# Earlier first loads, quarter folds and respaced folds in a fused attention and feed-forward kernel

## The chip, the cores and the metric

The kernel runs on one core of a Trainium2 chip. The metric is the device time of one execution in microseconds (us), taken as the median of several. A profile of one execution goes with each run; its span is about 1.8 us shorter than the time. All executions used here are with a granted TensorE clock of 0.99 to 1.00 of full speed.

## The reference

For each of four batches, `q`, `k`, `v` are 5824 x 256. The channels attend to each other, and the result goes through a multiplicative feed-forward layer:

```python
qn = q / (norm(q, axis=1) + 1e-6);  kn = k / (norm(k, axis=1) + 1e-6)
a  = softmax(kn.T @ qn / tau)            # 256 x 256 per batch
x  = v @ a                               # 5824 x 256
out = ((x @ w1) * (x @ w2)) @ w3 @ w_out # w1, w2: 256 x 1024, w3: 1024 x 1024, w_out: 1024 x 256
```

## The kernel before

No `x` is made. `a` is folded into the weights, `Wf = a @ [w1, w2]` (eight "folds" of 512 columns per batch), and `W = w3 @ w_out` is made once (eight "w products"). Then each step is two products with v transposed, a cast by ScalarE, a multiplication by VectorE and the product with `W`. A chunk is eight steps over 512 rows; a batch has eleven full chunks and a small last one of 192 rows.

The softmax of batch n+1 needs all of its q and k. Their products (`G`) and square sums are spread between the steps of batch n; for batch 0 they stand at the start, behind the loads. An agenda says at which time of a modelled clock each piece of such side work is put between steps:

```python
def fold_mm(i, c2, tag="ab", on_act=None):        # one fold: matmuls c2 = 0 and 1, then its evacuation
    ...
    dst = Wf[n][:, c1, w, h * 512 : (h + 1) * 512]
    if on_act if on_act is not None else i % 2 == 0:
        nc.scalar.activation(out=dst, in_=st["fold", i], func=AF.Copy, scale=st["rs"][:, c1 : c1 + 1])
    else:
        nc.vector.tensor_scalar_mul(dst, st["fold", i], st["rs"][:, c1 : c1 + 1])
...
+ [(0.2, 15.5, sums)]                              # cost, time after the end of the products
+ [(0.43, 16.5 + 0.85 * i, lambda i=i: fold(i)) for i in range(8)]
...
# start of the program
busy(14)                                           # dummy matmuls
load_piece("k", 0, 0, (half,))                     # all loads by GpSimd, which casts to bf16
load_piece("q", 0, 0, (half,))
...
# agenda of batch b
for jt in range(FT):
    at(26.0 + 1.2 * jt, 0.87, lambda jt=jt: w_unit(jt))     # w products, batch 0 only
...
t0, t1 = 57.0, 115.5      # batch 0: products of the next batch from t0 to t1
t0, t1 = 16.0, 104.0      # later batches
```

Folds and the step products `a` and `b` share four PSUM buffers (`tag="ab"`).

## Time and profile before

| | before |
|---|---|
| time, median of the runs beside the change | 573.16 us |
| span of the profile | 571.7 us |
| TensorE busy | 559.4 us (98%) |
| last k piece of batch 0 lets TensorE go | 31.53 us |
| first real step product | 40.69 us |

The useful reading here is of what TensorE does *not* do. I call a hole the distance between the starts of two successive matmuls, less what the first needs (columns / 2.4 GHz + 2.5 ns, as the prediction has it; 215.8 ns for 512 columns, where the trace has 216.5). Summed by stage, holes tell where time is lost even when the busy share reads 98%. The prediction below shows the lines.

### The profile page before, as it was taken

How to read it: one execution, taken by the hardware profiler on the slowest of the kernel's cores; microseconds unless marked ns; L12 is line 12 of the kernel's file. 1: busy time of each engine (PE TensorE's matmuls, PEld its weight loads, DVE VectorE, ACT ScalarE, POOL GpSimd, SP SyncE). 2: the span in 40 equal slices, each digit the busy share in tenths (PEclk: the TensorE clock that was granted, in tenths of full speed). 3: DMA queues.
4: the chain of work that ended last, by engine and by line, in shares of the span. 5: the costliest groups of instructions: out<-in, count | busy, mean ns of one | idle time of the engine just before them, and what ended most of it. 6: DMA issues, size and time to landing. Idle time of an engine off the chain costs nothing.

```text
span 571.7 us, 10102 instructions
## 1 busy us (share of the span) xinstructions
PE 559.4 (98%) x3750; PEld 354.5 (62%) x3750; DVE 377.4 (66%) x612; ACT 337.7 (59%) x624; POOL 83.3 (15%) x164
## 2 busy tenths in 40 slices
PE   7789999999999999999999999999999999999997
PEld 4655576776666666666666666666665666666665
DVE  1047744788977567887776667778876656565564
ACT  0046644777856567776766567767766554454453
POOL 5250020303030111121030012031120000000000
PEclk9999999999999999999999999999999999999999
DMA  8999959869685697495661595665640325221011
GB/s 163 211 187 208 184 104 240 170 149 242 140 183 118 123 204 150 94 192 121 145 144 72 99 215 123 140 136 126 175 110 38 85 73 148 63 63 75 38 72 58
DMA packets 74560, 76.93 MB, mean 135 GB/s; under 512 B 54160, under 2 KB 58256, under 8 KB 74512
## 3 DMA queue, kind: packets, MB, share of 16 engines
q0 software_dynamic: 15504, 39.46, 39.3%
q1 hardware_dynamic: 58784, 36.64, 22.2%
q8 instruction: 29, 0.48, 0.3%
q10 hardware_dynamic: 224, 0.20, 0.1%
q14 instruction: 19, 0.16, 0.1%
HBM read 78.91 MB, written 23.86 MB: 180 GB/s over the span
## 4 chain that ended last, share of the span: by engine, by line
PE 92%; DMA 5%; DVE 1%; ACT 1%; POOL 1%; issue 0%; ACTq 0%; POOLq 0%
PE o L479 28%; PE a L438 27%; PE b L438 27%; PE G L188 5%; DMA k<-in_k_dram 5%; PE fold L349 2%; PE w L596 1%; ACT as L444 0%; ACT kr L279 0%; POOL k L109 0%; POOL q L109 0%; DVE abs L453 0%; PE sqk L221 0%; DVE vT L136 0%; DVE abs L455 0%
## 5 line engine op out<-in xcount | busy, mean ns | idle before, releaser
L453 DVE TENSOR_TENSOR abs<-as,b 128x512 bf16<-128x512 bf16 x336 | 230.5, 687 | 141.4 <-ACT as L444 130.3
L444 ACT CAST as<-a 128x512 bf16<-128x512 f32 (+1 forms) x384 | 216.1, 563 | 176.9 <-DVE abs L453 90.2
L438 PEld LDWEIGHTS <-Wf 128*128 128x128 bf16 x1536 | 149.2, 98 | 102.0 <-issue 1.9
L479 PE MATMUL o<-W_sb,abs 128*128 128x256 bf16 x1376 | 209.6, 273 | 0.1
L438 PE MATMUL a<-vT,Wf 128*128 128x512 bf16 x704 | 209.4, 379 | 0.2
L438 PE MATMUL b<-vT,Wf 128*128 128x512 bf16 x704 | 209.3, 379 | 0.0
L479 PEld LDWEIGHTS <-abs 128*128 128x128 bf16 x1376 | 134.5, 98 | 81.6 <-DVE abs L455 0.3
L197 DVE TENSOR_TENSOR acc<-acc,sq 128x1024 f32<-128x1024 f32 x66 | 80.4, 1219 | 0.4 <-ACT sq L185 0.3
L188 PE MATMUL G<-k,q 128*128 128x256 bf16 x276 | 49.9, 273 | 0.0
L185 ACT ACTIVATE sq<-q 128x512 f32<-128x512 bf16 x66 | 41.8, 634 | 0.0
L185 ACT ACTIVATE sq<-k 128x512 f32<-128x512 bf16 x66 | 41.6, 630 | 0.0
L426 POOL COPY gate_t<-abs 1x1 bf16<-1x1 bf16 x39 | 13.9, 355 | 167.7 <-DVE abs L453 167.0
L500 DVE COPY osb<-o 128x512 f32<-128x512 f32 x44 | 30.1, 685 | 0.7 <-PE o L479 0.7
L430 POOL COPY gate_t<-vT 1x1 bf16<-1x1 bf16 x17 | 4.4, 258 | 169.3 <-DMA vT<-v 134.0
L188 PEld LDWEIGHTS <-q 128*128 128x128 bf16 x276 | 27.0, 98 | 3.1
L499 ACT COPY osb<-o 128x512 f32<-128x512 f32 x44 | 25.8, 586 | 3.8 <-PE o L479 1.8
L279 ACT ACTIVATE kr<-row 128x256 f32<-128x256 f32 x1 | 0.4, 385 | 31.6 <-PE row L267 31.6
L109 POOL DMA_DIRECT2D q<-in_q_dram x29 | 15.7, 541 | 13.2 <-DMA k<-in_k_dram 6.0
L349 PE MATMUL fold<-w,e 128*128 128x512 bf16 x64 | 17.0, 380 | 0.5 <-DVE vT L136 0.4
L356 ACT ACTIVATE Wf<-fold,rs 128x512 bf16<-128x512 f32 x16 | 10.9, 688 | 8.1 <-PE fold L349 6.4
L244 DVE TENSOR_TENSOR dk<-sqk,ident 128x256 f32<-128x256 f32 x1 | 0.4, 425 | 21.3 <-PE sqk L221 21.3
L109 POOL DMA_DIRECT2D k<-in_k_dram x25 | 13.8, 551 | 3.7 <-DMA k<-in_k_dram 1.9
(89 smaller groups left out, 240.4 us busy)
## 6 DMA issues: line engine op xcount, KB each, us to landing
out_dram<-osb SPq DMA_DIRECT2D x44, 512.0 KB, 3.1
k<-in_k_dram POOLq DMA_DIRECT2D x19, 512.0 KB, 8.5
v<-in_v_dram POOLq DMA_DIRECT2D x19, 512.0 KB, 5.2
q<-in_q_dram POOLq DMA_DIRECT2D x18, 512.0 KB, 6.6
w_wout<-in_moe_w_dram POOLq DMA_DIRECT2D x1, 2048.0 KB, 23.6
k<-in_k_dram POOLq DMA_DIRECT2D x4, 320.0 KB, 9.9
v<-in_v_dram POOLq DMA_DIRECT2D x4, 320.0 KB, 5.4
q<-in_q_dram POOLq DMA_DIRECT2D x4, 256.0 KB, 12.0
```

The costliest lines, as they stand in the source:

```text
L109: nc.gpsimd.dma_start(out=pieces[nm, n, pi][:, lo:hi, :], in_=qk_main[nm, n][0][:, pi * PIECE + lo : pi * PIECE + hi, :])
L185: nc.scalar.activation(out=dst[:, :, part, :], in_=src[:, o : o + 2, :], func=AF.Square)
L188: nc.tensor.matmul(G[:, ct, :], lhsT=qt[:, i, ct * P : (ct + 1) * P], rhs=kt[:, i, :], start=(pr == 0 and part == 0 and ct == 0), stop=(pr ...
L197: nc.vector.tensor_add(accs[n], accs[n], sqs[0])
L349: nc.tensor.matmul(st["fold", i], lhsT=st["e"][:, c2, c1 * P : (c1 + 1) * P], rhs=w12[:, c2, w, h * 512 : (h + 1) * 512], start=(c2 == 0), ...
L426: nc.gpsimd.tensor_copy(gate_t, last_ab[0][:1, :1])
L438: nc.tensor.matmul(t[:, :n], lhsT=Wf[b][:, ct, w, j * P : (j + 1) * P], rhs=rhs_of(b, c, ct), start=(ct == 0), stop=(ct == CT - 1),)
L444: nc.scalar.copy(a_sb[:, :n], tiles[0][:, :n])
L453: nc.vector.tensor_mul(ab, a_sb, tiles[1])
L479: nc.tensor.matmul(tl[h][:, o, :], lhsT=lhsT, rhs=W_sb[:, j, :], start=(j == 0 and o == 0), stop=(j == FT - 1 and (small or o == 1)), skip ...
L499: nc.scalar.copy(o[:, 0:2, :], tl[0])
L500: nc.vector.tensor_copy(o[:, 2:4, :], tl[1])
```

## The change

Its intent: start the first loads earlier by giving half a piece of k and of q to SyncE, which is idle; fold only the columns that the first steps need before the first step and the rest between steps; load q and k of batch 1 earlier; and spread the folds at each change of batch so that their evacuations do not pile up. The core of the diff, condensed:

```diff
-            sum_mm(0) ... fold_mm(0..1), fold(2), transpose, fold(3), fold(4), fold(5)
+            sum_mm(0); quarters of columns 0:256 (both w, both c1); sum_mm(1)   # evacuated 128 columns at a time
+        def second_quarter(): ...                  # columns 256:512, after the first step
-            + [(0.2, 15.5, sums)]
-            + [(0.43, 16.5 + 0.85 * i, lambda i=i: fold(i)) for i in range(8)]
+            + [(0.2, 16.5, sums)]
+            + [(0.43, 17.5 + 1.1 * i, lambda i=i: fold(i)) for i in range(8)]
...
-    busy(14)
-    load_piece("k", 0, 0, (half,))
-    load_piece("q", 0, 0, (half,))
+    busy(10)
+    for nm in "kq":
+        new_piece(nm, 0, 0)
+        raw[nm] = work.tile([P, half, C], F32, tag="o_sb", name=f"raw_{nm}", bufs=3)
+        nc.sync.dma_start(out=raw[nm], in_=qk_main[nm, 0][0][:, :half, :])
+        load_part(nm, 0, 0, half, PIECE)
...
+    nc.vector.tensor_copy(pieces["k", 0, 0][:, :half, :], raw["k"])
+    nc.scalar.copy(pieces["q", 0, 0][:, :half, :], raw["q"])
...  # v first half piece, then w1 and w2 in columns 0:256, 256:512, 512:1024 (before: halves)
-    busy(4)
+    busy(3)
+    transpose_half_on_pe(0, 0, 0, False)
...
-                at(1.5 + 0.6 * i, 0.43, soft0[5 + i])
+            at(0.5, 0.87, soft0[5]);  at((1.7, 2.6, 3.5, 3.9)[i], 0.43, soft0[6 + i])
...  # moves: ("qk", 1, 0) at 29 ahead of ("v", 0, 3), ("qk", 1, 2) at 47, v(1, 0..2) 2 earlier
-            t0, t1 = 57.0, 115.5
+            t0, t1 = 54.0, 113.0
-            t0, t1 = 16.0, 104.0
+            t0, t1 = 16.0, 98.0
```

## The prediction

> **What bounds the kernel now.** I read the page first: the busy shares, the slices, and the chain that ended last.
>
> ```profile
> PE 559.4 (98%) x3750; PEld 354.5 (62%) x3750; DVE 377.4 (66%) x612; ACT 337.7 (59%) x624; POOL 83.3 (15%) x164
> ...
> PE   7789999999999999999999999999999999999997
> ...
> PEclk9999999999999999999999999999999999999999
> ...
> PE 92%; DMA 5%; DVE 1%; ACT 1%; POOL 1%; issue 0%; ACTq 0%; POOLq 0%
> ```
>
> TensorE is busy 98% of 571.7 us at full granted clock, and only the first three slices (43 us) and the last show slack. So any gain must come out of TensorE's few holes. To size them I took the start of each matmul in the timeline and subtracted the spacing that the one before needs. In full flow two 512-column matmuls start 0.433 us apart, so 0.2165 us each. The excess over that spacing sums to 13.1 us: 9.5 before 40 us, 0.95 at the first change of batch (175 to 182 us), 0.60 at the second (303 to 315), 1.47 at the third (436 to 448), 0.6 at the very end, and zero in every 10 us bucket between. So 3.0 us lie in the three changes and the rest in the start.
>
> The timeline of the start shows what holds it:
>
> ```profile
> 1.22 1.23 POOL L109 DMA_DIRECT2D k<-in_k_dram  x2 [0.78 <-POOLq L692]
> ...
> 31.53 0.84 PE L221 MATMUL sqk<-k 128*128 128x128 bf16 x12 [0.18 <-DMA k<-in_k_dram]
> ...
> 34.74 1.03 PE L209 MATMUL warm_I-482_483<-warm 128*128 128x512 bf16 x4
> ...
> 37.02 0.20 PE L328 MATMUL sum<-ones_b,e 128*128 128x1 bf16 x2 [1.25 <-ACT e L318]
> ...
> 40.69 0.59 PE L438 MATMUL a<-vT,Wf 128*128 128x512 bf16 x2
> ```
>
> GpSimd issues the first load at 1.22 us; the last k piece of batch 0 lets TensorE go at 31.53; the squares and products of what was left run to 34.7; four dummy matmuls and a wait fill the softmax chain to 37.02; six folds and one transpose of v run to 40.69, where the first real product starts. Windows of 2 to 4 us give the load's pace:
>
> ```profile
> 2.00:4.00 2.00, 2.00 (x6) 0.76 (x5) 0.00 (x0) 0.01 (x1) 2.00 (x5) 1.00 0.66 76
> 4.00:6.00 2.00, 2.00 (x9) 0.70 (x7) 0.00 (x0) 0.00 (x0) 2.00 (x5) 1.00 1.11 203
> ...
> 16.00:20.00 4.00, 2.14 (x26) 1.58 (x23) 0.00 (x0) 0.00 (x0) 0.56 (x1) 1.00 1.06 214
> ```
>
> The last two columns are DMA share and GB/s landed (bf16; twice that is read as fp32). From 4 to 28 us the rate is flat at 203 to 221, the DMA share over 1: the load is limited by transfer, not by issue or by TensorE. Summing packets gives 110 KiB landed at 4 us and 5257 KiB at 29, which is 206 KiB/us; that line drawn back meets zero at 3.48 us. So the load behaves as if it began at 3.48 us, and an earlier start moves the whole front end earlier.
>
> The third change of batch, the worst, in the timeline:
>
> ```profile
> 438.29 1.65 PE L349 MATMUL fold<-w,e 128*128 128x512 bf16 x6
> ...
> 446.60 0.33 PE L438 MATMUL a<-vTt,Wf 128*128 128x192 bf16 x2 [0.27 <-ACT as L444]
> ```
>
> Three folds back to back (six matmuls) come here and again 3 us later; this run takes 1.78 us from its start to the next matmul (438.29 to 440.07) where 6 x 0.2165 = 1.30 would do. Each fold must be evacuated (0.69 us on ScalarE, 0.75 on VectorE) from four shared PSUM buffers, and the backlog reaches the small last chunk, where TensorE needs less time per step than ScalarE and VectorE.
>
> **What the Trainium skill says.** "DMA: Bandwidth & Descriptors", section SWDGE vs HWDGE vs iDMA: casting in a DMA is GpSimd's alone. Hence raw fp32 by SyncE needs a cast on VectorE and ScalarE; no trace before shows that. Its Specifications give first-byte latencies of about 1 us (GpSimd) and 0.6 us (SyncE). The trace agrees in order, not in size: GpSimd's first issue at 1.22 has its first packet at 2.60 (1.38 us); SyncE's last full output store, issued at 564.40, has its first at 565.23 (0.83) and its last, of 512 KiB, at 566.66. Same page, Issuing engines are not separate DMA queues: all use the same 16 engines, so a second issuer adds no bandwidth. I take that as it stands: I credit the earlier start, not a higher rate. "TensorE: Matmul & The Clock Gate", section Wait — 56ns, not 53.3ns?: N / 2.4 GHz plus about 2.5 ns per matmul, 215.8 ns for 512 columns; the trace has 216.5.
>
> **The change part by part.**
>
> 1. First half pieces of k and q by SyncE. In the trace SyncE is released at 0.65 us and then has nothing to do. Issuing at about 0.7, plus 0.83, gives packets from about 1.55 us, 512 KiB of source in about 1.4 us. It fills the hole before 3.48: effective start 1.6 to 2.2 instead of 3.48, so 1.3 to 1.9 us less. The two casts (1024 columns; a VectorE add of that width is 1.22 us, a ScalarE copy 1.01) run while TensorE waits for loads, so they cost nothing. Credit: **-1.5 us**, for everything up to the last k piece. Ten warm-up matmuls instead of 14 lie under the load as well: 0.
>
> 2. Quarters first. TensorE's work is the same (eight 512-column matmuls become sixteen of 256: 8 x 2.5 ns more); only idle and filler count. Before, from 34.74 to 40.69: filler 4 x 0.2165 = 0.87, then a hole of 1.41 to 37.02, 0.1 at the sums, 0.51 at the fold that waited behind VectorE's vT copy: 2.9 us. After: filler 0.65, the v transpose (0.45) moved into the hole, which leaves 1.18, 0.1, and then TensorE has nothing to do between the last first-quarter matmul (about 38.0) and the first evacuated column block. That block needs the reciprocal sums (38.11 before) plus 0.07 plus one evacuation of 256 elements (about 0.45, from 0.69 for 512 and 0.42 for 256 columns on ScalarE), so 38.65: 0.65. Sum 2.6: **-0.3 us**. The first real product itself starts about two microseconds earlier, but work it jumped over comes back.
>
> 3. That work, the second quarter and folds 4 to 7, now lies between the first four product steps. I stepped the four PSUM buffers through with as 0.59, product 0.69, folds 0.69 and 0.75 us. Fold 7 waits about 0.3 us for a buffer, and product step 4, whose columns start at 512, waits about 0.5 for fold 7's evacuation. **+0.8 us**; before had no hole there. The w1, w2 quarters have the same bytes ahead of them as the halves had, so they should land in time with about half a microsecond to spare.
>
> 4. Folds spread, products of batches 1 and 2 ending at 98 instead of 104. The new order of instructions, which I built but did not run, has at the second and third change all eight folds inside the last full chunk, in pairs, with a product step between pairs and one after the sums; none stays for the small chunk. At the first change they go mostly one by one through the last chunk, with no run of three at the end. Of 3.0 us I keep 0.8 (0.18 at the leftover rows stays): **-2.2 us**. VectorE has room: the products get 82 clock units instead of 88, so its adds rise 7% where it is busy 74% (89.78 of 121.1 us, 182 to 303).
>
> 5. q and k of batch 1 ahead of late v: v piece 3 was transposed by 82.66 us and is first used at 107.04 us; a load of two pieces in front costs about 5 us of that 24. Piece 4: 105.4 against 139.6. The transfers stay hidden: **0**.
>
> Sum: -1.5 - 0.3 + 0.8 - 2.2 = **-3.2 us**. 572.96 - 3.2 = 569.8 us.
>
> **Rivals.** (a) The SyncE start gains nothing, because startup latency or a shared limit holds the first packets: for it, nobody has seen SyncE's first load here; against it, SyncE idle from 0.65 and a DMA hole until 3.5. Then 571.3. (b) Four PSUM buffers turn the early interleaved folds into holes of 2 us or more, as the runs of three do at the third change, or the w quarters with their short rows land late (the rate sinks to 131 to 188 KiB/us while short pieces land at 30 to 33 us): then 571 to 571.5. (c) The folds only move their holes into the last full chunk: gain there 0.5, total 571.5. (d) Everything works better, early holes near zero and changes of batch clean: 568.3. (e) A late v or q stalls a whole chunk: slower by several us; the slacks under 5 speak against it.
>
> **Range and chances.** Two rivals at once give about 572.5, the good case 568.3. Runs agree within 0.1% apart from one of 575.41 in three. I say 569.8, range 568.2 to 571.8. Two per cent is 11.5 us; the whole slack is 13.1 plus 1.5 of filler, much of it needed, so faster by that is all but excluded, and slower needs a stall that nothing shows.
>
> **What would show it.** Step 1: the last k piece releases TensorE near 30.0 instead of 31.53, first packets at 1.5 to 1.6. Step 2: the first product near 37.1 us (38.65 less 1.5) instead of 40.69. Step 3: waits of folds or products for evacuation between 39 and 46 us, near 0.8 us. Step 4: excess spacing at the three changes near 0.8 in total. Step 5: no TensorE wait for vT. The prediction is wrong if the load's end does not move, if the early holes pass 2 us, or if new holes open in mid-batch.

## The result, and the profile after

The changed kernel takes 572.23 us (median of six, 571.62 to 573.43) against 573.16 beside it. The ratio is 0.9979, 95% interval 0.996 to 0.9997. (Ratios are the mean time of one kernel's runs over that of the other's of the same rounds, so not quite the ratio of the medians quoted.) The gain is 0.9 us where I had forecast 3.2, and the time is above my range. In the changed kernel L438 has become L463, L479 L504 and L349 L350. First, three lines of its page: busy times and the chain that ended last.

```profile
PE 558.5 (98%) x3753; PEld 354.8 (62%) x3753; DVE 377.7 (66%) x613; ACT 339.9 (60%) x627; POOL 77.5 (14%) x164
...
PE 91%; DMA 6%; ACT 1%; DVE 1%; issue 0%; POOL 0%; ACTq 0%; POOLq 0%
PE o L504 27%; PE a L463 27%; PE b L463 27%; PE G L188 5%; DMA k<-in_k_dram 5%; PE fold L350 2%; DMA w3T<-w_wout 1%; PE w L627 1%; ACT as L469 1%; PE quarter L376 0%; ACT kr L279 0%; POOL k L109 0%; DVE s L313 0%; ACT e L318 0%; DVE abs L478 0%
```

The same bound, but a new item in the chain, `DMA w3T<-w_wout`: the transposes of w3, on nobody's path before. The timeline of the start:

```profile
0.73 0.40 SPq L542 DMA_DIRECT2D raw_k<-in_k_dram  x1
...
30.63 0.84 PE L221 MATMUL sqk<-k 128*128 128x128 bf16 x12 [0.17 <-DMA k<-in_k_dram]
...
35.88 0.20 PE L328 MATMUL sum<-ones_b,e 128*128 128x1 bf16 x2 [0.77 <-ACT e L318]
...
37.59 0.61 PE L463 MATMUL a<-vT,Wf 128*128 128x512 bf16 x2 [0.56 <-DVE Wf L387]
```

The last k piece lets TensorE go 0.90 us earlier, and the first step product starts 3.1 us earlier. The lead is spent later. The table gives the holes by stage for every profile; "early" runs from the first step product to the w products, "1st", "2nd" and "3rd" are the changes of batch. In some profiles a few matmul records are missing; each missing fold matmul (0.216 us) is taken out of the holes, and so are the four one-column matmuls of the sums at each change (0.09 us).

| run | last k | first step | early | w products | 1st | 2nd | 3rd | span | median time |
|---|---|---|---|---|---|---|---|---|---|
| before | 31.53 | 40.69 | 0.00 | 0.00 | 0.94 | 0.60 | 1.48 | 571.7 | 573.16 |
| changed | 30.63 | 37.59 | 0.25 | 0.65 | 1.60 | 0.24 | 0.60 | 570.5 | 572.23 |
| e1 SyncE alone | 30.97 | 39.61 | 0.12 | 0.00 | 0.94 | 0.60 | 1.19 | 570.3 | 572.26 |
| e2 dummy first | 31.49 | 40.64 | 0.00 | 0.00 | 0.94 | 0.60 | 1.47 | 571.5 | 572.96 |
| e3 w late | 30.87 | 37.89 | 0.21 | 0.00 | 1.60 | 0.24 | 0.60 | 570.0 | 572.04 |
| e4 products to 105 | 30.50 | 37.46 | 0.21 | 0.08 | 0.60 | 0.37 | 0.60 | 578.4 | 577.22 |
| e5 w late, old batch 0 | 30.50 | 37.46 | 0.22 | 0.00 | 1.90 | 0.24 | 0.61 | 569.9 | 571.92 |
| e6 without SyncE | 31.52 | 38.55 | 0.08 | 0.00 | 1.60 | 0.25 | 0.60 | 570.7 | 572.75 |
| e7 fold times alone | 31.43 | 40.46 | 0.00 | 0.00 | 0.36 | 0.42 | 0.60 | 569.7 | 571.49 |
| e8 w1, w2 in halves | 30.89 | 37.95 | 0.21 | 0.00 | 1.60 | 0.24 | 0.61 | 570.2 | 573.06 |
| e9 folds deferred | 30.24 | 37.68 | 0.22 | 0.08 | 3.12 | 0.47 | 0.61 | 571.9 | 572.41 |
| e10 folds at end, v later | 30.60 | 38.10 | 0.21 | 0.00 | 0.36 | 0.24 | 0.61 | 569.0 | 570.49 |
| e11 SyncE and fold times | 30.70 | 39.65 | 0.12 | 0.00 | 0.36 | 0.24 | 0.61 | 568.8 | 571.46 |
| e12 folds at end | 30.57 | 37.53 | 0.21 | 0.00 | 0.36 | 0.24 | 0.60 | 568.5 | 570.50 |
| e13 folds alone later | 30.35 | 37.77 | 0.21 | 0.00 | 0.76 | 0.24 | 0.61 | 569.1 | 571.04 |
| e14 folds at end, halves | 30.44 | 38.26 | 0.21 | 0.00 | 0.36 | 0.24 | 0.61 | 569.2 | 571.24 |

Every profile has 0.60 us more at the end of the last batch. The holes and the release by the last k piece repeat well between profiles except where a transfer is involved: the last k piece varies from 30.24 to 30.97 in the twelve runs with SyncE (mean 30.6; 31.5 in the four without), and in e9, e10 and e13 a q piece comes later still and costs 0.6 us. The medians are of four different rounds; the kernel before beside them had 573.01 to 573.55.

The third change of the changed kernel, to be compared with the run of three in the prediction: four matmuls, 4 x 0.2165 = 0.87 us, and the next product after 0.87.

```profile
436.90 1.03 PE L350 MATMUL fold<-w,e 128*128 128x512 bf16 x4
437.77 0.59 PE L463 MATMUL a<-vT,Wf 128*128 128x512 bf16 x2
```

The balance of the change in its profile: last k piece -0.90; from there to the first step, holes and filler from 3.25 to 2.76, -0.49; early +0.25; w products +0.65; changes of batch +0.66, -0.36, -0.88. Sum -1.1 us; the spans differ by 1.2.

### The profile page after: what moved, and what is told of

It reads as the page before. It is cut to its first block, busy times and chain, and to the rows that moved or that the text cites. A ratio compares the mean times of both kernels' runs of the same rounds, so it can differ in the third digit from the quotient of the medians.

```text
span 570.5 us, 10131 instructions
## 1 busy us (share of the span) xinstructions
PE 558.5 (98%) x3753; PEld 354.8 (62%) x3753; DVE 377.7 (66%) x613; ACT 339.9 (60%) x627; POOL 77.5 (14%) x164
## 4 chain that ended last, share of the span: by engine, by line
PE 91%; DMA 6%; ACT 1%; DVE 1%; issue 0%; POOL 0%; ACTq 0%; POOLq 0%
PE o L504 27%; PE a L463 27%; PE b L463 27%; PE G L188 5%; DMA k<-in_k_dram 5%; PE fold L350 2%; DMA w3T<-w_wout 1%; PE w L627 1%; ACT as L469 1%; PE quarter L376 0%; ACT kr L279 0%; POOL k L109 0%; DVE s L313 0%; ACT e L318 0%; DVE abs L478 0%
## 5 line engine op out<-in xcount | busy, mean ns | idle before, releaser
L463 PEld LDWEIGHTS <-Wf 128*128 128x128 bf16 x1536 | 149.0, 98 | 102.8 <-issue 2.3
L463 PE MATMUL a<-vT,Wf 128*128 128x512 bf16 x704 | 209.4, 379 | 0.8 <-DVE Wf L387 0.6
L504 PE MATMUL o<-W_sb,abs 128*128 128x256 bf16 x1376 | 209.9, 273 | 0.1
L463 PE MATMUL b<-vT,Wf 128*128 128x512 bf16 x704 | 209.4, 379 | 0.0
L504 PEld LDWEIGHTS <-abs 128*128 128x128 bf16 x1376 | 134.5, 98 | 81.9 <-DVE abs L480 0.3
L451 POOL COPY gate_t<-abs 1x1 bf16<-1x1 bf16 x39 | 9.6, 246 | 171.8 <-DVE abs L478 171.0
L350 PE MATMUL fold<-w,e 128*128 128x512 bf16 x56 | 15.0, 379 | 0.2 <-ACT as L469 0.2
L478 DVE TENSOR_TENSOR abq<-as,b 128x512 bf16<-128x512 bf16 x16 | 10.8, 687 | 5.2 <-ACT as L469 4.6
```

The lines of the kernel that those rows point to most:

```text
L350: nc.tensor.matmul(m, lhsT=st["e"][:, c2, c1 * P : (c1 + 1) * P], rhs=w12[:, c2, w, lo:hi], start=(c2 == 0), stop=(c2 == CT - 1),)
L463: nc.tensor.matmul(t[:, :n], lhsT=Wf[b][:, ct, w, j * P : (j + 1) * P], rhs=rhs_of(b, c, ct), start=(ct == 0), stop=(ct == CT - 1),)
L478: nc.vector.tensor_mul(ab, a_sb, tiles[1])
L504: nc.tensor.matmul(tl[h][:, o, :], lhsT=lhsT, rhs=W_sb[:, j, :], start=(j == 0 and o == 0), stop=(j == FT - 1 and (small or o == 1)), skip ...
```

## The experiments

Edits are shown condensed. The w products first, for the new item in the chain. What TensorE's weight loads waited for in the changed kernel (time in all, times, longest), and a piece of its chain in order of time:

```profile
PEld L627 <- DMA w3T<-w_wout: 1.3, 2, 0.7
```

```profile
62.53 5.76 DMA w3T<-w_wout
68.29 0.04 issue
68.34 1.92 PE w L627 x16
```

The w products wait for transposes of w3. Before, TensorE came to them at 67.07 us, now at 64.2, and the transposes started no earlier: 60.46 us in this profile, 59.85 before.

**e1: SyncE loads alone** (the kernel before with only this part):

```diff
-    load_piece("k", 0, 0, (half,)); load_piece("q", 0, 0, (half,))
+    ... raw fp32 halves by nc.sync, second halves by load_part, casts on VectorE and ScalarE
```

> The kernel before with only the SyncE loads of the first half pieces (and the two casts) added. Theory of the ramp: the load's start-up is moved with the first packet and not removed, so the last k piece releases TensorE at about 30.6 us (31.53 before, 30.63 in the changed kernel), the first packets come at about 1.8 us, GpSimd's first packets only near 4.9, and the first product near 39.8. Rival, as I predicted it: SyncE fills the whole hole and the release is at 30.0; it was then something else in the changed kernel that cost 0.6 us. Time about 0.9 us below before.

Release at 30.97, first packets at 1.75 us, GpSimd's first at 4.79, first step at 39.61, time 572.26 against 573.11. By the medians this part alone brings what the whole change brings (0.85 us); with one of four executions at 573.86 the ratio is 0.9993, 0.9977 to 1.001, so times alone do not show it. Its lead of about a microsecond at the first step is kept to the end in the profile. The rival of a release at 30.0 falls.

Only 0.56 us of that lead is the release. The rest is the hole of 0.51 us between two folds at 39.09 us, which is gone in e1. The prediction put it down to VectorE's copy of vT; the weight load of the waiting fold names the load of w1 and w2. First the kernel before, then e1:

```profile
39.81 0.55 PEld L349 LDWEIGHTS <-e 128*128 128x128 bf16 x4 [0.84 <-DMA w<-in_moe_w_dram]
```

```profile
38.31 1.46 PE L349 MATMUL fold<-w,e 128*128 128x512 bf16 x6
38.51 0.69 DVE L136 COPY vT<-tr_I-515_516 128x1024 bf16<-128x1024 bf16 x1
```

In e1 the third and fourth of these matmuls, the same fold, run while the copy goes on, so the copy does not hold it.

The windows of the changed kernel show why the release came so late; to be compared with those of before in the prediction (last two columns: DMA share, GB/s landed; SyncE's fp32 counts in full, GpSimd's casts as half):

```profile
0.00:2.00 2.00, 0.76 (x2) 0.28 (x3) 0.94 (x6) 1.27 (x1) 0.97 (x6) 1.00 0.24 23
2.00:4.00 2.00, 2.00 (x6) 0.76 (x5) 0.00 (x0) 0.01 (x1) 2.00 (x5) 1.00 0.81 281
```

SyncE moves data before 2 us, yet slowly: its packets before 2 us take 699 ns each on average, as GpSimd's before 3 us do in the kernel before (694), against 144 to 155 in the third microsecond of traffic. (These first means vary: 350 to 776 ns over the runs with SyncE.) Counted in bytes of source landed, the line through 10 and 28 us, drawn back, meets zero at 2.83 us instead of 3.67. That shift, 0.84 us (0.65 to 0.84 by the stretch chosen), is about the shift of the first packet (2.60 to 1.77). My credit of 1.5 us had treated SyncE's first packet as the start of full rate, while I had measured GpSimd's start on the full-rate line, which includes its slow microsecond.

**e2: one small dummy load by SyncE, first** (nobody reads it):

```diff
+    early = work.tile([P, 64], F32, tag="early", name="early", bufs=1)
+    nc.sync.dma_start(out=early, in_=qk_main["k", 0][0][:, 0, :64])
```

> The kernel before with one 32 KiB load by SyncE into a tile that nobody reads, issued first; all real loads stay with GpSimd. If the slow first packets (about 700 ns each, for a microsecond) belong to the first traffic of the core whoever issues it, the dummy takes them on itself, GpSimd's first packets run at 150 to 200 ns each and the release of TensorE by the last k piece comes 0.5 to 0.9 us earlier than 31.53. If they belong to GpSimd's own queue, nothing moves: 31.5.

Nothing moves: release at 31.49, GpSimd's first packets at 2.60 and still 543 ns each on average (434 to 694 in the three profiles where GpSimd loads alone). A small transfer by another issuer does not take the slow start on itself. Whether the slow start belongs to the queue or to the first large transfer stays open: in e1 GpSimd's own first packets, coming after SyncE's megabyte, take 172 ns at once.

**e3: w products later:**

```diff
-                at(26.0 + 1.2 * jt, 0.87, lambda jt=jt: w_unit(jt))
+                at(29.0 + 1.2 * jt, 0.87, lambda jt=jt: w_unit(jt))
```

> The changed kernel with the eight products of w3 and w_out placed 3 units later in batch 0 (29 instead of 26). Theory: TensorE reached them 2.7 us earlier than in the kernel before while the transposes of w3 come no earlier, so the two holes at 64.0 and 67.9 us (0.38 + 0.24 us) are waits for those transposes and vanish; the time falls by about 0.6 us. Rival: the holes come from PSUM buffers held by the product casts (the page names ScalarE's cast as the releaser) and stay, moved by 3 us; time unchanged.

The holes there are gone and the rest of the table stays; in the profile 0.5 us of span go with a release 0.24 later. The median, 572.04, is only 0.2 below the changed kernel's, and one of four executions took 574.32. So the rival of PSUM buffers falls, but this hole is not in every execution: in e13, which has the w products at the old place, the transposes happened to start at 58.98 and there is none. With the same loads the start varies from 58.98 to 60.46. The hole appears when it is late.

**e8: w1 and w2 in halves, as before the change:**

```diff
-    for f0, f1 in ((0, 256), (256, 512), (512, F)):
+    for f0, f1 in ((0, 512), (512, F)):
```

> The changed kernel with w1 and w2 loaded in two halves of 512 columns instead of two quarters and a half. Theory: the 1 KiB rows of the quarters slow the load stream between 33 and 37 us and use up the lead that SyncE gave, so with halves the first transpose of w3 starts at about 59.9 or earlier instead of 60.46 and the holes at the w products shrink from 0.65 to about 0.1; the first quarter's products do not wait, since the same bytes are ahead of them. Rival: the w3 load is as late with halves (it is limited elsewhere), the holes stay at 0.65.

The same window of the changed kernel, then of e8:

```profile
34.00:36.00 2.00, 1.23 (x15) 0.75 (x13) 1.73 (x9) 1.50 (x6) 2.00 (x5) 1.00 0.92 111
```

```profile
34.00:36.00 2.00, 1.35 (x14) 0.81 (x11) 1.65 (x9) 1.43 (x5) 2.00 (x3) 1.00 1.22 181
```

With quarters (rows of 512 bytes in SBUF) the stream moves 111 GB/s here, with halves 181. This pair is an extreme one: over all profiles the window has 108 to 176 with quarters and 141 to 185 with halves. The packets are steadier: one of 512 bytes takes 60 ns (median, every profile), one of 1 KiB 98, so the same bytes take longer in quarters. The transposes of w3 start at 58.46 us and the holes are gone with the w products at the old place. In the runs with SyncE they start at 58.10 to 58.89 us with halves (e1, e8, e11, e14) and at 58.98 to 60.46 with quarters (eight runs): the quarters use up the lead that SyncE gave. Why e6, quarters without SyncE, starts at 59.71, no later than halves without it (59.76 to 60.29), is open. The time did not show the gain: 573.06, with executions from 572.11 to 574.55.

**e4: products and folds of batch 0 earlier**, so that its folds fall into the last full chunk:

```diff
-            t0, t1 = 54.0, 113.0
+            t0, t1 = 50.0, 105.0
```

> The changed kernel with the next batch's products in batch 0 between 50 and 105 instead of 54 and 113, so that the folds fall into the last full chunk as they do in batches 1 and 2. Theory: the 1.6 us of holes at the first change of batch (170 to 182 us) come from folds and small product steps sharing ScalarE and VectorE in the small chunk, and shrink to 0.3 to 0.6 as at the other changes; time down by about 1 us. Rival: batch 0 is too full for it, and the denser squares and sums open holes of the same size between 90 and 150 us; time unchanged.

The first change falls to 0.60 us, as the theory had it, but 9.6 us of holes open before it in the profile (of the slowest execution, 580.54), and the median is 4.1 us worse. Here the rival wins in size and not in cause. TensorE's waits in this run:

```profile
PE G L188 <- DMA k<-in_k_dram: 7.3, 2, 5.1
```

The products wait for k pieces. GpSimd issues these loads in order, behind waits for the transposes of v. That is why the products of batch 1 have to be late.

**e5: w products late, old times of batch 0:**

```diff
+   w_unit at 29;  n == 1: sums 15.5, folds 16.5 + 0.85 * i;  t0, t1 = 57.0, 115.5
```

> The changed kernel with the w products 3 units later and, in batch 0 alone, the old times of products (57 to 115.5) and folds (0.85 apart). Theory: the first change of batch goes back from 1.60 us of holes to the 0.94 of the kernel before, the holes at the w products (0.65) are gone, the others stay at 0.24 and 0.60; time about 571.0. Rival: with TensorE earlier by 3 us the small chunk of batch 0 has 1.6 us of holes whatever the spacing; then about 571.7.

571.92 us, but the first change did not return to 0.94: it is 1.90. Of these, 0.51 is a single hole at 165.4 us, where ScalarE waits 1.5 us for GpSimd's all-reduce of the square sums and the casts of the steps stand behind it. The old times do not mean the old place: with quarters the agenda's clock also counts side work that used to come before it, so each entry falls earlier among the steps.

**e6: the changed kernel without the SyncE part:**

```diff
-    raw fp32 halves by nc.sync, load_part(nm, 0, 0, half, PIECE), and the two casts
+    load_piece("k", 0, 0, (half,))
+    load_piece("q", 0, 0, (half,))
```

> The changed kernel with all loads by GpSimd as before (the SyncE part alone undone). Theory: the release by the last k piece goes back to about 31.5 us, the first product to about 38.4, and since TensorE is then later, the holes at the w products shrink, so the net cost of undoing is only some 0.3 to 0.9 us: 572.5 to 573.1. Rival: if the SyncE part were worth its 0.9 us in full in this company, 573.1 and holes at the w products as large as with it (0.65).

Release at 31.52, no holes at the w products, 1.60 at the first change, 572.75 us. In this company SyncE's 0.9 us is worth 0.2 of span (570.7 against 570.5), because TensorE then gets to the w products 0.9 us later and does not wait. The 1.60 us at the first change do not come from the earlier start.

**e7: fold times alone** (the kernel before with these lines):

```diff
-            + [(0.2, 15.5, sums)] + [(0.43, 16.5 + 0.85 * i, ...)]
+            + [(0.2, 16.5, sums)] + [(0.43, 17.5 + 1.1 * i, ...)]
-            t0, t1 = 16.0, 104.0
+            t0, t1 = 16.0, 98.0
```

> The kernel before with only the folds spread (1.1 instead of 0.85 apart, sums a unit later, in all batches) and products to 98 instead of 104 in batches 1 and 2. Theory: holes at the three changes go from 0.94, 0.60, 1.48 to about 1.2 (or more), 0.24, 0.60, as in the changed kernel, so the gain is near 1.0 us from the second and third and the first gives some back; time about 572.3. Rival: the gain at the second and third change depends on the earlier start and is not there alone.

571.49 against 573.01, ratio 0.9971 (0.9956 to 0.9986): better than the whole change. The second and third change gain as foreseen, and the first does not get worse but falls from 0.94 to 0.36. In its instruction order only two folds stand between small steps there; the other six come in a row at the very end of the batch.

**e9: four folds deferred into the next batch** (the last four of batch 1's weights at 0.9, 1.8, 2.7 and 3.2 of batch 1; w products late):

```diff
+        for i, (cst, fn) in enumerate(late): at((0.9, 1.8, 2.7, 3.2)[i], cst, fn)
+            if b == 0 and i >= len(soft) - 4: late.append((cst, fn)); continue
```

> The changed kernel with the w products 3 units later and the last four folds of batch 1's weights (columns 512 to 1023, first needed at its fifth product step) moved out of the small last chunk of batch 0 into the first three steps of batch 1, as the change does at the start of batch 0. Theory: the holes at the first change fall from 1.60 to 0.5 us or less, those at the w products are gone: time about 570.6, 2.5 us below before. Rival: the first steps of batch 1 cannot hold four folds without holes and the 1.6 us reappear after 182 us: 571.6.

Inconclusive for its question. The profile fell on a slow execution (573.77; the others 571.40 to 573.01). Its waits between 158 and 182 us:

```profile
ACT kr L279 <- POOL tot L258: 3.2, 1, 3.2
```

The late all-reduce again, now with a hole of 1.47 us on TensorE; it hides what the deferral is worth. One thing can be read: the four folds stand between steps of batch 1 (182.56 to 186.56 us) without a hole, so in this profile the rival falls.

**e10 and e12: folds of batch 0 at the end.** Both have the w products at 29; e10 also loads v piece 2 behind the all-reduce.

```diff
-            t0, t1 = 54.0, 113.0
+            t0, t1 = 57.0, 117.2
-            ... ("v", 1, 2, 114.0)
+            ... ("v", 1, 2, 120.5)      # e10 only
```

> The changed kernel with the w products 3 units later, the products of batch 0 to 57 and 117.2 (so that the instruction order at the first change is that of the agenda-only run: two folds between the last small steps, six in a row at the end) and the load of v piece 2 of batch 1 moved behind the all-reduce on GpSimd. Theory: holes at the first change are set by folds between small product steps, not by folds in a row, and fall from 1.60 to about 0.4 us; w products 0; time about 570.6 (2.4 below before). Rival: the first change costs 1.6 us or more whenever TensorE is ahead of the loads by 3 us, because ScalarE waits for a late all-reduce; then 571.6.

> As the one with the folds at the end of batch 0, but with v piece 2 loaded ahead of the all-reduce, as in the changed kernel. Theory: GpSimd waits for the transpose of v piece 1 before it can start the all-reduce, ScalarE waits for the all-reduce and with it the product casts, and the holes at the first change are larger than with v behind it: 0.5 to 2 us against 0.4. Rival: the all-reduce is in time anyway and both runs have the same holes.

Both 570.5 us (ratios 0.9948, 0.9929 to 0.9967, and 0.9946, 0.9922 to 0.9969), 2.7 below the kernel before, and 0.36 us at the first change. So the order of v and the all-reduce is nothing here, and e12's expectation fails in favour of its rival. These are the best versions found. The timeline of TensorE at the first change, first the changed kernel, then e12:

```profile
178.66 0.27 PE L504 MATMUL o<-W_sb,abs 128*128 128x256 bf16 x1
179.02 0.32 PE L463 MATMUL a<-vTt,Wf 128*128 128x192 bf16 x2
179.18 0.33 PE L463 MATMUL b<-vTt,Wf 128*128 128x192 bf16 x2
179.35 0.27 PE L504 MATMUL o<-W_sb,abs 128*128 128x256 bf16 x1
179.79 0.59 PE L350 MATMUL fold<-w,e 128*128 128x512 bf16 x2 [0.18 <-ACT as L469]
```

```profile
177.62 0.27 PE L504 MATMUL o<-W_sb,abs 128*128 128x256 bf16 x1
177.73 2.75 PE L350 MATMUL fold<-w,e 128*128 128x512 bf16 x12
180.32 0.59 PE L463 MATMUL a<-vT,Wf 128*128 128x512 bf16 x2
```

An `o` matmul of 256 columns takes 0.11 us to the next start, as at 177.62. In the changed kernel it takes 0.36 at 178.66 and 0.44 at 179.35: the next product or fold waits for a PSUM buffer that ScalarE has not emptied. In e12 six folds run in a row without a hole: 12 x 0.2165 = 2.60 us, and 2.59 measured. In a row, evacuations alternate between ScalarE (0.69 us) and VectorE (0.75), about 0.36 per fold, less than the 0.43 that TensorE takes for one. Between small steps they share both engines with a cast (0.32) and two multiplications (0.29 + 0.22) per step. That it is this sharing is argued from these durations; that it is the place of the folds is shown (e13 below). A run in a row is no cure by itself: the three in the prediction, between full steps with a cast of 0.59 and a multiplication of 0.69, cost 0.48 us.

**e11: SyncE and fold times together, no quarters** (the kernel before with both parts):

```diff
+    raw fp32 halves by nc.sync, load_part(nm, 0, 0, half, PIECE), and the two casts   # as e1
+            + [(0.2, 16.5, sums)] + [(0.43, 17.5 + 1.1 * i, ...)];  t0, t1 = 16.0, 98.0   # as e7
```

> The kernel before with the SyncE loads and the spread folds, but without the quarters and with batch 0's old times for everything else. Theory: the two gains measured alone, 0.9 and 1.5 us, add up since nothing here runs 3 us ahead of the loads: holes at the changes 0.4, 0.4, 0.6 and none at the w products, time about 570.6 to 570.8. Rival: part of the earlier start is lost again at the w products or at the first change; then 571.5.

The profile adds up as the theory says (568.8 us of span, 570.61 us for that execution). The median of 571.46 comes from two groups: three executions at 570.6 to 570.8 and three at 572.2 to 573.0. What the slower ones do is not seen. In span e12 is only 0.3 us ahead of e11 (568.5 against 568.8), so in these profiles quarters, which e11 lacks, are worth little once the folds stand well. The medians are 1.0 apart, by e11's slower group. No run has the quarters alone.

**e13: sums and folds of the first change alone later:**

```diff
+            n == 1: sums at 20.7, folds at 21.7 + 1.1 * i
```

> The changed kernel with only the sums and folds at the first change moved 4.2 units later, so that six folds stand in a row at the end of batch 0, while products and softmax chain stay where the change put them (w products not moved either, so 0.65 us of holes there stay). Theory: most of the 1.60 us, those holes after 174 us (1.25 us), come from folds between small steps and go, 0.3 stay there; the 0.35 us hole at 170.3, where ScalarE's cast waits behind an exponential, stays: first change 0.6 to 0.7 in all, time about 571.3. Rival: it is the place of the chain; then the first change stays above 1.2 us and the time at 572.

The first change falls from 1.60 to 0.76 us with products and softmax chain where the change put them; 0.35 stay at 169.8 us, where the cast stands behind an exponential on ScalarE, and 0.34 in the small chunk. So the place of the folds makes 0.84 us, and the place of the chain the other 0.4 down to e12. The time, 571.04, is below the changed kernel's also because this execution had no hole at the w products.

**e14: folds at the end and halves** (e12 with these lines):

```diff
-    for f0, f1 in ((0, 256), (256, 512), (512, F)):
+    for f0, f1 in ((0, 512), (512, F)):
-                at(29.0 + 1.2 * jt, ...)
+                at(26.0 + 1.2 * jt, ...)
```

> The changed kernel with batch 0's products to 57 and 117.2 and w1 and w2 in halves, w products at the old time. Theory: the halves alone make the w3 transposes early enough, so holes at the w products are 0 to 0.1 us, at the first change 0.36, the time equals that of the run with late w products, 570.5. Rival: with TensorE as early as this the halves are not always in time and a hole of 0.2 us or more shows at 64 us.

No holes at the w products, as expected. But the first step comes 0.73 us later than in e12, and so does the end (569.2 against 568.5); the time is 571.24. A new hole of 0.44 us stands between the first quarter's matmuls, at 36.17 us, where they wait for w: the halves move the wait to the start. Another 0.42 is a VectorE add in the softmax chain (L304, two columns): 0.58 us here, 0.16 in e12, 0.40 in the kernel before. Where it is long it ends within 0.01 us of one of GpSimd's DMA issues (35.31 and 35.32 here). That GpSimd's issue holds it was not tested.

## Why the prediction was wrong

**Step 4** (folds spread, forecast -2.2 us) failed, and it is the largest error: the changes of batch gave -0.58. Its sentence "at the first change they go mostly one by one through the last chunk, with no run of three at the end" took that for an advantage. The runs showed the reverse. Folds between small steps cost (1.60 us; 0.76 when they alone are moved), folds in a row at the end of the batch do not (e12). At the second and third change the forecast held: 0.60 and 1.48 became 0.24 and 0.60, and e7 shows that this gain stands alone. That I blamed the runs of three for the holes before was half the story: the small chunk was the other half.

**Step 5** (reordered loads, forecast 0) was right for v and for q and k: no wait for vT appeared. But it checked only the transfers that the diff moved. TensorE came 2.8 us earlier to the w products, and the transfer that was not moved, w3 with its transposes, became a wait of 0.65 us in the profiled execution: the new hole in mid-batch that the prediction named as a sign of being wrong.

**Step 1** (SyncE, forecast -1.5) had the right mechanism and the wrong size: -0.90 in the changed kernel, -0.56 in e1's profile, -0.9 between the means of the profiles with SyncE and without. The mis-sized term is the effective start, 1.6 to 2.2 us forecast and 2.72 measured on the prediction's own line (528 KiB of source landed at 4 us, 10847 at 29), because SyncE's own slow first microsecond was left out and its first packet came 1.04 us after the issue (0.73 to 1.77) and not 0.83.

**Step 2** (quarters first, forecast -0.3) measured -0.49, partly by luck: the hole before the sums is 0.94 and not 1.18 because the VectorE add of e14 takes 0.16 us here instead of 0.40, which nobody foresaw. Its 0.51 was a wait for w1 and w2 and not for the vT copy (e1); it went away all the same. The first step is at 37.59 against my 37.1, late by the error of step 1 less this add. **Step 3** (early folds, forecast +0.8) measured +0.25, of which 0.08 lies between 39 and 46 us, where the forecast had it, and 0.13 is a hole at 54.8 us that e1 has without quarters. My stepping let each buffer go later than it does; the hole before product step 4 did not appear. So steps 2 and 3 came out 0.7 us better than forecast and hid a part of the misses of 1.6 (step 4), 0.65 (step 5) and 0.6 (step 1).

Of the rivals, (c) came closest: the folds moved their holes, though into the small chunk of batch 0 and not into a full one. Rival (b)'s warning of short rows came true as lost lead and not as a wait at the folds. The time is near the 572.5 that the prediction gave for two rivals at once.

## What to carry to other kernels

Earlier work is worth only what the next thing it meets can take: before crediting a lead, list every transfer that the leading engine will reach, also those that the change does not touch. Put evacuation-heavy side work where the evacuating engines have slack, and ask it of each place by itself; spreading it evenly is not the same. A start-up measured on a rate line includes its slow ramp, so compare first packet with first packet, or line with line, and never one with the other.

## What the Trainium skill lacked or had wrong

- "DMA: Bandwidth & Descriptors", Specifications, gives first-byte latencies of about 0.6 us (SyncE) and 1 us (GpSimd) and no slow start after them. Here SyncE's first load took 1.04 us from issue to first packet and GpSimd's 1.38, the first packets took about 700 ns each in the two kernels compared, against 150 to 200 later, and full rate came about 1.4 us after the first packet (first packet 2.60, full rate from 4 us in the kernel before).
- The same page, Queues, rings and completion order, says that each DMA engine goes round-robin between its queues packet by packet. In the changed kernel GpSimd's first packet comes at 4.90 us although its load was issued at 1.22 (2.60 when alone): between 4 and 5 us SyncE has 105 packets and GpSimd 3. No such interleaving shows in that stretch. But the page's packet holds several descriptors (9 to 17), and SyncE's two loads have 18 records in the trace for each DMA engine, so one turn at most was to be seen; whether GpSimd's packets were ready earlier is not seen.
- The same page, Specifications, gives 512 bytes as the least size for line rate. In GpSimd's casting loads between 28 and 42 us of the kernel before, packets of 512 bytes landed take 60 ns (median), of 1 KiB 98, of 2 KiB 173 and of 4 KiB 324: 8.5 bytes per ns at 512 and 12.6 at 4 KiB.
